# A retention layer and an MLP in one kernel, rebuilt: attention units across batches, groups of 512 with the two MLP layers in turn, Strassen products in the second layer, and gated loads

## The chip, the cores and the metric

The kernel runs on one core of one Trainium2 chip. The metric is device microseconds of one execution, as the median of several runs. An engine is named as the profile names it: PE is TensorE (PEld its weight loads), DVE is VectorE, ACT is ScalarE, POOL is GpSimd, SP is the engine that issues DMAs.

## The reference

Eight batches of 576 tokens with eight heads of 64 go through a retention layer (attention scores with a decay of gamma to the distance, causal, no softmax), and the result, as 4608 rows of 512, goes through an MLP with a leaky relu.

```python
scores = scale * np.matmul(q, k.transpose(0, 1, 3, 2))       # q, k, v: (8, 8, 576, 64) f32
gamma = 1.0 - 2.0 ** (-5.0 - np.arange(H))
Dmat = np.where(rel >= 0, gamma[:, None, None] ** rel, 0.0)  # rel = row - column
ret = scores * Dmat
attn = np.matmul(ret, v)
x = attn.transpose(0, 2, 1, 3).reshape(B * S, H * D)         # (4608, 512)
h = x @ w_in                                                 # w_in: (512, 2048)
g = np.maximum(0.01 * h, h)
return g @ w_out                                             # w_out: (2048, 512)
```

## The kernel before

Retention is computed in chunks of 64 tokens, two chunks to a unit. A unit never crosses a batch, and 576 = 4 x 128 + 64, so each batch has four full units and one of 64 rows: 40 units. For a unit, q and v are multiplied by powers of gamma (so the decay inside a block of 256 needs only a causal mask), everything is cast to f16, and q and k are transposed: on PE for units 0 to 6, by a DMA transpose from unit 7 on.

```python
def cast_qk(u):
    ...
    nc.scalar.copy(out=t[0:n, 1], in_=t32[u, 1][0:n])                       # k, on ACT
    (nc.vector if u < NEARLY else nc.gpsimd).tensor_tensor(... op=MUL)      # q times its decay
    if u >= NPE:                                                            # NPE = 7, NEARLY = 8
        nc.sync.dma_start_transpose(out=qkT[u]..., in_=t[0:n]...)
def cast_v(u):      # the same for v, DVE or POOL
...
def scores(u):      # q k^T per chunk and head, and k^T v (the chunk's state): up to 32 matmuls of 64x64
def masks(u):       # DVE: causal mask on the scores, to f16
def states(u):      # DVE: adds the chunk states up; then the cast to f16:
    (nc.scalar.copy if u < NEARLY else nc.gpsimd.tensor_copy)(out=st16[u], in_=s32)
def outputs(u):     # 32 matmuls of 64x64: own chunk ("own") and earlier chunks ("far");
    nc.scalar.copy(out=tmp..., in_=own...)                                  # ACT
    for o in range(2):
        for c in range(2):
            nc.vector.tensor_tensor(out=xT[half(o), ps, ...], in0=far..., in1=tmp..., op=ADD)
```

From unit 7 on, one step does the burst of one unit and the casts of the unit two ahead:

```python
def steady(n):
    def go():
        if NRING < n + 4 < NU:
            loads(n + 4, nc.sync)
        if n < NU:
            scores(n)
        if n > NFIRST:
            outputs(n - 1)
        if n < NU:
            masks(n)
            states(n)
        casts(n + 2)
```

The MLP works on groups of tokens, three of 256, seven of 512 and one of 256. The first layer of a group is interleaved with the second layer of the group before, and steps are spread over them so that the group after has its x in time. All matmuls of the MLP have 128x128 weights; the second layer streams 512 columns.

```python
sizes = [256] * 3 + [512] * 7 + [256]
...
def g1_blocks(g):           # first layer: hps += w_in[:, c, f]^T xT, leaky relu on ACT to f16
def g2_blocks(g, width=1):  # second layer:
    ...
    nc.tensor.matmul(out=y_cur[g, tb], lhsT=g_tiles[g][:, f, tb * P : (tb + 1) * P],
                     rhs=w_out16[:, f, :], start=(f == 0), stop=(f == NF - 1))
    ...
    nc.vector.tensor_copy(out=osb, in_=y_cur[g, tb])
    nc.sync.dma_start(out=out[r0 : r0 + P, :], in_=osb)
...
run(ends[3], g1[2] + g2_blocks(2))
run(ends[4], g1_blocks(3))
for g in range(4, NG):
    run(ends[g + 1], g1_blocks(g), g2_blocks(g - 1))
run(ends[NG], g2_blocks(NG - 1))
```

The first 12 units and the weights are loaded almost wholly from POOL's queue, in the order of its instructions (the weights are cast from f32 to f16 on the way), the later units from SP's.

Of the kernel before, what the change touches and what calls it, by code (L numbers as in the profile page):

```python
# [12 lines left out]
ADD = mybir.AluOpType.add  # L13
PSUM = bass.MemoryType.PSUM
# [3 lines left out]
def kernel(  # L18
# [9 lines left out]

# [10 lines left out]
    XR = NT // 2  # L51
# [3 lines left out]
    tab = np.zeros((P, 2, 2, H))  # L55
    for w in range(2):
        r = (P * w + np.arange(P))[:, None] - BLK / 2
        tab[:, w, 0] = gamma[None, :] ** r * scale
        tab[:, w, 1] = gamma[None, :] ** (-r)
# [9 lines left out]
    NTAB = 2 * 2 * H  # L69
# [3 lines left out]
    a_pool = ctx.enter_context(tc.tile_pool(name="ap", bufs=4))  # L73
    g_pool = ctx.enter_context(tc.tile_pool(name="gp", bufs=2))
    o_pool = ctx.enter_context(tc.tile_pool(name="op", bufs=4))
    sc_pool = ctx.enter_context(tc.tile_pool(name="scp", bufs=1, space=PSUM))
    ot_pool = ctx.enter_context(tc.tile_pool(name="otp", bufs=1, space=PSUM))
    h_pool = ctx.enter_context(tc.tile_pool(name="hpp", bufs=2, space=PSUM))
    y_pool = ctx.enter_context(tc.tile_pool(name="yp", bufs=2, space=PSUM))

    ctx.enter_context(tc.manual_schedule())

    cs = const_pool.tile([P, consts.shape[1]], FP, name="cs")
    ident = const_pool.tile([P, P], F16, name="ident")
    nc.scalar.dma_start(out=cs, in_=c_dram.ap())
    nc.scalar.dma_start(out=ident, in_=i_dram.ap())
    tab_sb = cs[:, 0:NTAB].rearrange("p (w x h) -> p w x h", w=2, x=2)
# [3 lines left out]
    xT = const_pool.tile([P, NP, XR], F16, name="xT")  # L91
    w_in16 = const_pool.tile([P, NP, DFF], F16, name="w_in16")
    w_out16 = const_pool.tile([P, NF, DM], F16, name="w_out16")
    zst = const_pool.tile([P, NP, CH], F16, name="zst")

    units = [(b, w) for b in range(B) for w in range((S + P - 1) // P)]
    NU = len(units)
    nrows = [min(P, S - P * w) for b, w in units]
    NPE = 7
    NFIRST = 7  # L100
    NEARLY = 8
    NRING = 11
    t32 = {}
    qk16 = {}
    v16 = {}
    qkT = {}
    s16s = {}
    st16 = {}
    carry = {}
# [4 lines left out]
    def swap(p):  # L114
        return 1 if p >= NP // 2 else 0

    def load(u, x, eng):
        b, w = units[u]
        n = nrows[u]
        t = ld_pool.tile([P, H, D], FP, name=f"t32_{x}")  # L120
        t32[u, x] = t
        eng.dma_start(  # L122
            out=t[0:n],
            in_=(q, k, v)[x][b, :, P * w : P * w + n, :].rearrange("h t d -> t h d"),
        )

    def loads(u, eng):
        for x in (1, 0, 2):
            load(u, x, eng)

    def cast_qk(u):

        if u >= NU:
            return
        b, w = units[u]
        n = nrows[u]
        t = a_pool.tile([P, 2, H, D], F16, name="qk16")
        qk16[u] = t
        nc.scalar.copy(out=t[0:n, 1], in_=t32[u, 1][0:n])  # L139
        (nc.vector if u < NEARLY else nc.gpsimd).tensor_tensor(  # L140
            out=t[0:n, 0],
            in0=t32[u, 0][0:n],
            in1=tab_sb[0:n, w % 2, 0, :].unsqueeze(2).to_broadcast([n, H, D]),
            op=MUL,
        )
        if u >= NPE:
            qkT[u] = a_pool.tile([P, 2, NP, P], F16, name="qkT")
            nc.sync.dma_start_transpose(  # L148
                out=qkT[u][:, :, :, 0:n].rearrange("p x c t -> p (x c) t"),
                in_=t[0:n].rearrange("t x h d -> t (x h d)"),  # L150
            )

    def cast_v(u):
        if u >= NU:
            return
        b, w = units[u]
        n = nrows[u]
        t = a_pool.tile([P, H, D], F16, name="v16")
        v16[u] = t
        (nc.vector if u < NEARLY else nc.gpsimd).tensor_tensor(  # L160
            out=t[0:n],
            in0=t32[u, 2][0:n],
            in1=tab_sb[0:n, w % 2, 1, :].unsqueeze(2).to_broadcast([n, H, D]),
            op=MUL,
        )

    def casts(u):
        cast_qk(u)
        cast_v(u)

    def transposes(u, pool=None):

        n = nrows[u]
        qkT[u] = a_pool.tile([P, 2, NP, P], F16, name="qkT")
        if pool is None:
            trs = [y_pool.tile([P, NP, P], F16, name="yps") for x in range(2)]
        else:
            both = pool.tile([P, 2, 2 * NP, P], F16, name="sc")
            trs = [both[:, x, 0:NP, :] for x in range(2)]
        for x in (1, 0):  # L180
            for p in range(NP):
                nc.tensor.transpose(  # L182
                    trs[x][:, p, 0:n],
                    qk16[u][0:n, x, 2 * p : 2 * p + 2, :].rearrange("t h d -> t (h d)"),
                    ident[0:n, 0:n],
                )
            (nc.scalar.copy if x else nc.vector.tensor_copy)(
                out=qkT[u][:, x, :, 0:n], in_=trs[x][:, :, 0:n]
            )

    sc_tiles = {}

    def scores(u):

        nb = nrows[u] // CH
        a = sc_pool.tile([P, 2, 2, NP, CH], FP, name="sc")
        sc_tiles[u] = a
        for p in range(NP):
            for g in range(2):
                for j in range(nb):  # L200
                    nc.tensor.matmul(  # L201
                        out=a[half(j), g, 0, p, :],
                        lhsT=qkT[u][half(g), 1, p, half(j)],
                        rhs=qkT[u][half(g), 0, p, half(j)],
                        start=True, stop=True, skip_group_check=True,
                    )
        if nb == 2:
            for p in range(NP):
                for j in range(2):
                    for g in range(2):  # L210
                        nc.tensor.matmul(  # L211
                            out=a[half(g), j, 1, p, :],
                            lhsT=qk16[u][half(j), 1, 2 * p + g, :],
                            rhs=v16[u][half(j), 2 * p + g, :],
                            start=True, stop=True, skip_group_check=True,
                        )

    def masks(u):
        n = nrows[u]
        s16s[u] = a_pool.tile([P, 2, NP, CH], F16, name="s16")  # L220
        nc.vector.tensor_tensor(  # L221
            out=s16s[u][0:n],
            in0=sc_tiles[u][0:n, :, 0],
            in1=mask_sb[0:n].unsqueeze(1).unsqueeze(1).to_broadcast([n, 2, NP, CH]),
            op=MUL,
        )

    def states(u):
        b, w = units[u]
        if nrows[u] < P:  # L230
            return
        st = sc_tiles[u][:, :, 1]
        s32 = a_pool.tile([P, 2, NP, CH], FP, name="s32")
        if w == 0:
            nc.vector.tensor_copy(out=s32[:, 0], in_=st[:, 0])
        else:
            nc.vector.tensor_tensor(out=s32[:, 0], in0=st[:, 0], in1=carry[b], op=ADD)
        if w % 2 == 0:
            nc.vector.tensor_tensor(out=s32[:, 1], in0=st[:, 1], in1=s32[:, 0], op=ADD)
        else:  # L240
            tmp = a_pool.tile([P, NP, CH], FP, name="stmp")
            nc.vector.tensor_tensor(out=tmp, in0=st[:, 1], in1=s32[:, 0], op=ADD)
            nc.vector.tensor_tensor(  # L243
                out=s32[:, 1], in0=tmp,
                in1=gblk_sb.unsqueeze(2).to_broadcast([P, NP, CH]), op=MUL,
            )
        carry[b] = s32[:, 1]
        st16[u] = a_pool.tile([P, 2, NP, CH], F16, name="st16")
        (nc.scalar.copy if u < NEARLY else nc.gpsimd.tensor_copy)(out=st16[u], in_=s32)  # L249

    def st_before(u, j):
        if j:
            return st16[u][:, 0]
        return st16[u - 1][:, 1] if units[u][1] else zst

    def outputs_acc(u):

        n = nrows[u]
        b, w = units[u]
        ot = ot_pool.tile([P, 2, 2 * NP, CH], FP, name="ot")  # L260
        o_all = ot[:, 0].rearrange("q (p j) t -> q p j t", j=2)
        seen = set()
        for r in range(2):
            if r:
                nc.tensor.drain()
            for p in range(NP):
                for hh in range(2):
                    o = hh ^ swap(p)
                    nc.tensor.matmul(
                        out=o_all[half(o), p, r, :],  # L270
                        lhsT=v16[u][half(r), 2 * p + hh, :],
                        rhs=s16s[u][half(r), hh, p, :],
                        start=o not in seen, stop=False, skip_group_check=True,
                    )
                    seen.add(o)
            for j in range(2):
                if w == 0 and j == 0:
                    continue
# [347 lines left out]
```

## Time and profile before

| What | Value |
|---|---|
| median of 3 runs | 337.14 us (334.98 to 345.53) |
| span of the profiled run | 337.3 us |
| PE busy | 299.5 us, 89% |
| DVE, ACT, POOL busy | 147.8, 135.6, 122.0 us |
| bytes moved by DMA | 50.32 MB |
| first-layer matmuls (L428) | 704, of which 256 stream 256 columns |
| second-layer matmuls (L451, L496) | 512 and 64, all of 512 columns |

A page of the profile gives the busy time of each engine, the span in 40 slices with a digit of tenths for each engine, the DMA queues, the chain of work that ended last, and the costliest groups of instructions by line of the kernel. In a timeline, a line has a start, a duration, the engine and line, what is written and read, and a count; "[2.11 <-DMA qkT<-qk]" means that the engine had idled for 2.11 us until that DMA landed. Matmuls are pipelined, so their durations overlap: the pace is read from the distance of starts. "issue" in a chain is time in which the engine waited for nothing that the profile shows.

### The profile page before, as it was taken

How to read it: one execution, taken by the hardware profiler on the slowest of the kernel's cores; microseconds unless marked ns; L12 is line 12 of the kernel's file. 1: busy time of each engine (PE TensorE's matmuls, PEld its weight loads, DVE VectorE, ACT ScalarE, POOL GpSimd, SP SyncE). 2: the span in 40 equal slices, each digit the busy share in tenths (PEclk: the TensorE clock that was granted, in tenths of full speed). 3: DMA queues.
4: the chain of work that ended last, by engine and by line, in shares of the span. 5: the costliest groups of instructions: out<-in, count | busy, mean ns of one | idle time of the engine just before them, and what ended most of it. 6: DMA issues, size and time to landing. Idle time of an engine off the chain costs nothing.

```text
span 337.3 us, 8449 instructions
## 1 busy us (share of the span) xinstructions
PE 299.5 (89%) x3578; PEld 154.7 (46%) x3578; DVE 147.8 (44%) x326; ACT 135.6 (40%) x240; POOL 122.0 (36%) x148
## 2 busy tenths in 40 slices
PE   1798887595775699999999999999999999999995
PEld 0476643263332344444444444444444444445652
DVE  2670444945564336434453556354436553101011
ACT  3355631164153454444453545444444433332220
POOL 8786745605355333530540355035413510000000
PEclk9999799989997779999999999999999999999999
DMA  7999999879999986866779599968697211000111
GB/s 175 214 194 189 228 231 178 197 150 176 165 244 198 162 161 142 175 144 165 160 139 192 130 189 210 217 148 158 149 214 109 66 47 61 35 33 31 62 64 62
DMA packets 122982, 50.32 MB, mean 149 GB/s; under 512 B 112192, under 2 KB 116288, under 8 KB 122944
## 3 DMA queue, kind: packets, MB, share of 16 engines
q1 hardware_dynamic: 115632, 37.11, 54.8%
q0 software_dynamic: 7024, 12.59, 19.6%
q8 instruction: 28, 0.46, 0.6%
q10 hardware_dynamic: 288, 0.08, 0.1%
q14 instruction: 10, 0.08, 0.1%
HBM read 36.78 MB, written 9.44 MB: 137 GB/s over the span
## 4 chain that ended last, share of the span: by engine, by line
PE 65%; DMA 13%; issue 10%; POOL 9%; SPq 1%; DVE 0%; POOLq 0%
PE yps L451 31%; PE hps L428 29%; DMA t<-in_v_dram 6%; DMA w_out<-in_moe_w_out_dram 5%; POOL t L122 3%; POOL v L160 2%; POOL qk L140 2%; DMA qkT<-qk 2%; PE sc L201 2%; POOL w_in L343 2%; PE ot L313 1%; PE ot L303 1%; PE sc L211 1%; SPq L122 1%; SPq L148 0%
## 5 line engine op out<-in xcount | busy, mean ns | idle before, releaser
L428 PE MATMUL hps<-xT,w_in 128*128 128x512 f16 (+1 forms) x704 | 151.2, 352 | 3.6 <-DVE osb L505 3.4
L435 ACT ACTIVATE gt<-hps 128x512 f16<-128x512 f32 x144 | 85.6, 596 | 128.0 <-PE hps L428 127.8
L451 PE MATMUL yps<-w_out,gt 128*128 128x512 f16 x512 | 127.9, 379 | 0.0
L428 PEld LDWEIGHTS <-w_in 128*128 128x128 f16 x704 | 68.8, 101 | 62.7 <-issue 9.6
L327 DVE TENSOR_TENSOR xT<-ot,own 64x256 f16<-64x256 f32 (+1 forms) x144 | 50.3, 388 | 85.8 <-ACT own L321 85.3
L451 PEld LDWEIGHTS <-gt 128*128 128x128 f16 x512 | 49.1, 98 | 56.4
L249 POOL CAST st<-s 128x512 f16<-128x512 f32 x25 | 15.3, 610 | 135.3 <-DVE s L243 68.6
L461 DVE COPY osb<-yps 128x512 f32<-128x512 f32 x32 | 21.9, 687 | 69.9 <-PE yps L451 69.9
L321 ACT COPY own<-ot 128x512 f32<-128x512 f32 (+1 forms) x36 | 19.4, 538 | 38.2 <-PE ot L313 34.8
L140 POOL TENSOR_TENSOR qk<-t,cs 128x512 f16<-128x512 f32 (+1 forms) x32 | 33.4, 1043 | 0.1
L160 POOL TENSOR_TENSOR v<-t,cs 128x512 f16<-128x512 f32 (+1 forms) x32 | 33.4, 1042 | 0.0
L221 DVE TENSOR_TENSOR s<-sc,cs 128x512 f16<-128x512 f32 (+1 forms) x40 | 27.5, 689 | 5.0 <-PE sc L211 4.0
L139 ACT CAST qk<-t 128x512 f16<-128x512 f32 (+1 forms) x40 | 24.7, 620 | 7.4 <-DMA t<-in_k_dram 7.4
L201 PE MATMUL sc<-qkT 64*64 64x64 f16 x576 | 13.5, 205 | 14.6 <-DMA qkT<-qk 11.2
L201 PEld LDWEIGHTS <-qkT 64*64 64x64 f16 x576 | 9.0, 113 | 30.5 <-DMA qkT<-qk 17.2
L182 PE MATMUL yps<-ident,qk 128*128 128x128 f16 (+1 forms) x48 | 5.9, 274 | 11.3 <-ACT qk L139 8.4
L140 DVE TENSOR_TENSOR qk<-t,cs 128x512 f16<-128x512 f32 (+1 forms) x8 | 7.9, 986 | 18.0 <-DMA t<-in_q_dram 18.0
L313 PE MATMUL ot<-qkT,st 64*64 64x64 f16 x456 | 11.8, 197 | 2.2 <-ACT st L249 1.6
L303 PE MATMUL ot<-s,v 64*64 64x64 f16 x512 | 11.7, 197 | 0.3 <-DVE s L221 0.3
L122 POOL DMA_DIRECT2D t<-in_q_dram x12 | 10.5, 877 | 3.8 <-DVE qk L140 1.9
L122 POOL DMA_DIRECT2D t<-in_v_dram x12 | 10.2, 851 | 4.3 <-DMA t<-in_k_dram 1.5
L182 PEld LDWEIGHTS <-qk 128*128 128x128 f16 (+1 forms) x56 | 4.4, 119 | 16.1 <-ACT qk L139 11.1
(42 smaller groups left out, 152.8 us busy)
## 6 DMA issues: line engine op xcount, KB each, us to landing
out_dram<-osb SPq DMA_DIRECT2D x36, 256.0 KB, 2.3
t<-in_k_dram SPq DMA_DIRECT2D x23, 256.0 KB, 3.8
t<-in_q_dram SPq DMA_DIRECT2D x22, 256.0 KB, 4.5
t<-in_v_dram SPq DMA_DIRECT2D x22, 256.0 KB, 4.8
t<-in_q_dram POOLq DMA_DIRECT2D x10, 256.0 KB, 7.8
t<-in_v_dram POOLq DMA_DIRECT2D x10, 256.0 KB, 8.2
t<-in_k_dram POOLq DMA_DIRECT2D x9, 256.0 KB, 8.0
w_in<-in_moe_w_in_dram POOLq DMA_DIRECT2D x16, 128.0 KB, 6.0
```

The costliest lines, as they stand in the source:

```text
L122: eng.dma_start(out=t[0:n], in_=(q, k, v)[x][b, :, P * w : P * w + n, :].rearrange("h t d -> t h d"),)
L139: nc.scalar.copy(out=t[0:n, 1], in_=t32[u, 1][0:n])
L140: (nc.vector if u < NEARLY else nc.gpsimd).tensor_tensor(out=t[0:n, 0], in0=t32[u, 0][0:n], in1=tab_sb[0:n, w % 2, 0, :].unsqueeze(2).to_b ...
L160: (nc.vector if u < NEARLY else nc.gpsimd).tensor_tensor(out=t[0:n], in0=t32[u, 2][0:n], in1=tab_sb[0:n, w % 2, 1, :].unsqueeze(2).to_broa ...
L201: nc.tensor.matmul(out=a[half(j), g, 0, p, :], lhsT=qkT[u][half(g), 1, p, half(j)], rhs=qkT[u][half(g), 0, p, half(j)], start=True, stop=T ...
L221: nc.vector.tensor_tensor(out=s16s[u][0:n], in0=sc_tiles[u][0:n, :, 0], in1=mask_sb[0:n].unsqueeze(1).unsqueeze(1).to_broadcast([n, 2, NP, ...
L321: nc.scalar.copy(out=tmp[:, :, 0:nb, :], in_=own[:, 0:nb].rearrange("q j p t -> q p j t"))
L327: nc.vector.tensor_tensor(out=xT[half(o), ps, t0 : t0 + n].rearrange("q p (j t) -> q p j t", t=CH), in0=far[half(o), o ^ c, :, 0:nb, :], i ...
L428: nc.tensor.matmul(out=hps[:, f, :], lhsT=w_in16[:, c, fc * P : (fc + 1) * P], rhs=xT[:, c, t0 % XR : t0 % XR + tok], start=(c == 0), stop ...
L435: nc.scalar.activation(out=g_tiles[g][:, fb * nf : (fb + 1) * nf, :], in_=hps, func=mybir.ActivationFunctionType.Lrelu,)
L451: nc.tensor.matmul(out=y_cur[g, tb], lhsT=g_tiles[g][:, f, tb * P : (tb + 1) * P], rhs=w_out16[:, f, :], start=(f == 0), stop=(f == NF - 1),)
L461: nc.vector.tensor_copy(out=osb, in_=y_cur[g, tb])
```

## The change

The kernel is written anew around the same helpers. It consists of five parts.

1. Units are 128 tokens of the flat sequence of 4608 tokens, 36 of them. A unit may hold the last chunk of one batch and the first of the next; the table of decays has a row for each such kind, and the last chunk's state isn't kept. The pairs of heads are laid out so that one DVE instruction adds "far" and "own" for a unit.
2. Every group is 512 tokens, four units. A group's first layer runs in full, then its second layer; the bursts of the units that the next group needs stand at fixed places between.
3. The second layer of groups 1 to 8 is a Strassen product (in Winograd's form): g (512 x 2048) and w_out (2048 x 512) are cut into 2 x 2 parts, and seven products of 256 x 1024 by 1024 x 256 take the place of eight. The sums of w_out's parts are made once, the sums of g's parts for each group, both on DVE in f16. Group 0 does its second layer as before.
4. All units are loaded from SP's queue, all weights from POOL's, and each queue has loads that wait for a load of the other ("behind").
5. PE does the transposes up to unit 9.

What it is for: fewer columns through PE in the second layer, fewer and larger instructions on the other engines, and a start in which weights and units land in the order of their use.

```diff
-    units = [(b, w) for b in range(B) for w in range((S + P - 1) // P)]
-    NPE = 7
+    NG = NT // TOK
+    NU = NT // P
+    NPE = 10
...
+    def behind(dma, *others):          # dma starts after others have landed
...
+    load(4, w_in_loads[2])
+    o_loads = [load_w_out(0, (last_load[4, 0],)), load_w_out(1)]
+    load(5, o_loads[0])
+    o_loads += [load_w_out(2, (last_load[5, 0],)), load_w_out(3)]
...
+    load(6, o_loads[2])
...
-        for o in range(2):
-            for c in range(2):
-                nc.vector.tensor_tensor(out=xT[half(o), ps, ...], in0=far..., in1=tmp..., op=ADD)
+        nc.vector.tensor_tensor(out=xT[g]..., in0=ot_tiles[u][:, :, NP : 2 * NP]..., in1=owns[u]..., op=ADD)
...
+    def mix(g, n, x):                  # x: half of the 8 blocks, 4 x 256 elements
+        z, a, b, op = (
+            (s[:, 0], g_part(g, 1, 0), g_part(g, 1, 1), ADD),
+            (s[:, 1], s[:, 0], g_part(g, 0, 0), SUB),
+            (g_part(g, 1, 0), g_part(g, 0, 0), g_part(g, 1, 0), SUB),
+            (g_part(g, 0, 0), g_part(g, 0, 1), s[:, 1], SUB),
+        )[n]
+        nc.vector.tensor_tensor(out=z[:, fs], in0=a[:, fs], in1=b[:, fs], op=op)
...
+        def product(name, lhs, rhs, fresh):     # 16 matmuls of 256 columns
+            ...
+            for n, (f, tb) in enumerate(order):
+                nc.tensor.matmul(out=r[name][:, tb, :], lhsT=lhs[:, f, tb * P : (tb + 1) * P],
+                                 rhs=rhs[:, f, :], start=fresh and n == 0, stop=f == HF - 1, ...)
...
+        plan = (
+            ("p1", g_part(g, 0, 0), w_part(0, 0), True, lambda: keep("k1", "p1")),
+            ("p1", g_part(g, 0, 1), w_part(1, 0), False, lambda: give(0, 0, "p1")),
+            ("p6", s[:, 1], w_mix[:, 1], True, lambda: keep("u2", "p6", "k1")),
+            ("p5", s[:, 0], w_mix[:, 0], True, lambda: keep("v", "p5", "u2")),
+            ("p7", g_part(g, 1, 0), w_mix[:, 2], True, lambda: give(1, 1, "p7", "v")),
+            ("p5", g_part(g, 0, 0), w_part(1, 1), False, lambda: give(0, 1, "p5", "u2")),
+            ("p7", g_part(g, 1, 1), w_mix[:, 3], False, lambda: give(1, 0, "p7", "u2", 2 if last else 1)),
+        )
...
+    def step(u):
+        burst(u)                       # scores(u), outputs(u - 1), masks, states, state cast, add
+        fetch(u + 3)
+        ahead(u + 2)                   # casts (k on ACT, q and v on POOL) and the DMA transpose
...
+    for g in range(2, NG):
+        more = g < NG - 1
+        for n, f in enumerate(first + second):
+            h_block(g, f)
+            if more and n in (4, 12):
+                step(4 * g + 5 + (n == 12))
+            if n == 8:
+                for m in range(3):
+                    mix(g, m, 0)
+        for m in range(3):
+            mix(g, m, 1)
+        seven(g, {0: [lambda: step(4 * g + 7)], 4: [lambda: step(4 * g + 8)]} if more else {}, g == NG - 1)
```

In the plan, a product with True starts a fresh accumulator and one with False adds to what stands in PSUM, after the reading of it that is named there ("keep" copies to SBUF, "give" to the output rows; with two names it adds on DVE, with one it copies on ACT). Before group 2, the order is written out by hand: units 0 to 3 with PE transposes, the first layer of group 0 in pieces as w_in's quarters arrive, its second layer in four parts as w_out's quarters arrive, with units 4 and 5 between them; then the first layer of group 1 with units 6 to 10.

## The prediction

> **What bounds the kernel now.** I read the page's busy table and slices first, then the windows by stage, then the PE timeline for the pace of each kind of matmul, and last the chain of waits where PE has holes.
>
> ```profile
> PE 299.5 (89%) x3578; PEld 154.7 (46%) x3578; DVE 147.8 (44%) x326; ACT 135.6 (40%) x240; POOL 122.0 (36%) x148
> PE   1798887595775699999999999999999999999995
> PEclk9999799989997779999999999999999999999999
> GB/s 175 214 194 189 228 231 178 197 150 176 165 244 198 162 161 142 175 144 165 160 139 192 130 189 210 217 148 158 149 214 109 66 47 61 35 33 31 62 64 62
> ```
>
> The reader is to see two stages. From slice 15 on (a slice is 8.4 us) PE never drops below 9; before it PE has holes, at a clock that is mostly full. The windows put the border at 116 us:
>
> ```profile
> 72.00:116.00 44.00, 29.44 (x596) 16.48 (x600) 23.57 (x57) 18.28 (x34) 19.68 (x22) 0.95 1.14 179
> 116.00:337.00 221.00, 217.36 (x2288) 104.64 (x2276) 90.17 (x202) 88.70 (x156) 55.62 (x63) 0.99 0.59 126
> ```
>
> (Columns: busy PE, PEld, DVE, ACT, POOL, granted clock, DMA share, GB/s.) After 116 us the end is set by PE alone: 217 of 221 us, and the rest is the last store. So what counts there is the pace of a matmul. Starts in the timeline of PE give it:
>
> ```profile
> 306.35 1.04 PE L428 MATMUL hps<-xT,w_in 128*128 128x256 f16 x8
> 307.22 1.89 PE L451 MATMUL yps<-w_out,gt 128*128 128x512 f16 x8
> 308.95 1.04 PE L428 MATMUL hps<-xT,w_in 128*128 128x256 f16 x8
> ```
>
> Eight matmuls of 256 columns take 307.22 - 306.35 = 0.87 us, 109 ns each, and eight of 512 take 1.73 us, 216 ns each. Each has its own weight load (PE and PEld both count 3578), so a load of 128 columns hides even behind 256. The burst of one attention unit:
>
> ```profile
> 194.96 1.03 PE L451 MATMUL yps<-w_out,gt 128*128 128x512 f16 x4
> 195.92 0.32 PE L201 MATMUL sc<-qkT 64*64 64x64 f16 x16
> ...
> 196.56 1.04 PE L428 MATMUL hps<-xT,w_in 128*128 128x512 f16 x4
> ```
>
> Four matmuls from 194.96 end their issue at 195.82; the next starts at 196.56. A burst of 64 small matmuls costs 0.73 us.
>
> Before 116 us the chain of waits is another one:
>
> ```profile
> 80.80 1.00 POOL v L160
> 81.80 4.01 issue
> 85.83 0.08 POOL st L249
> 86.40 1.04 POOL qk L140
> 87.44 1.00 POOL v L160
> 88.44 4.14 issue
> ```
>
> ```profile
> 85.83 0.61 POOL L249 CAST st<-s 128x512 f16<-128x512 f32 x1 [4.03 <-DVE s L239]
> 87.59 0.32 PE L201 MATMUL sc<-qkT 64*64 64x64 f16 x16 [2.11 <-DMA qkT<-qk]
> ```
>
> It is a loop through a unit's stations: POOL casts q and v (2.1 us), SP issues the DMA transpose (median 1.26 us, 3.3 us to landing), PE does the scores, DVE masks and states, POOL's state cast waits for DVE, and POOL's next casts stand behind it. Score bursts start at 72.1, 76.7, 82.2, 87.6 and on to 115.4: 5.4 us a unit. The MLP work placed between them, 40 matmuls of 256 columns and 76 of 512, is 4.4 + 16.4 = 20.8 us, with nine bursts 27 us of the 44. By 116 us the old kernel has scored 17 units, about 2,000 tokens, though its MLP has finished 768 and is in the first layer of the next 512. The loss is run-ahead: attention at its loop's pace with too little MLP between.
>
> **What the Trainium skill says.** "TensorE: Matmul & The Clock Gate", section "Back-to-back issue gap", gives N/2.4 + 2.5 ns for warm matmuls: 109.2 ns at 256 columns and 216 at 512, which is what the trace shows (109, 216). The same section's 131 ns for N=512 in a stream with weight loads is contradicted by the 216. "VectorE: DVE Perf Modes", section "The perf-mode tier table (the rule you actually need)", has tensor_tensor at twice the rate when all operands are 16-bit in SBUF (1224 ns for 2048 elements), once otherwise; the trace has only f32 or PSUM forms, 690 ns for 512 elements. From that page I estimate 0.69 us for a 1024-element f16 add or subtract, and 1.22 us if the fast mode fails. "DMA: Bandwidth & Descriptors", section "Issuing engines are not separate DMA queues", says that queues of different engines share the same 16 DMA engines; so the two cross-gated queues bring order, not bandwidth. The trace has both queues active in the first 60 us at about 200 GB/s, and doesn't separate them.
>
> **The change, part by part.**
>
> Strassen in the second layer: a group of 512 tokens was 64 matmuls of 512 columns, 64 x 216 = 13.8 us. It becomes seven products of 16 matmuls of 256 columns, 112 x 109 = 12.2 us. This holds for groups 1 to 8: 8 x 1.6 = 13 us less on PE, all on the path. It adds on DVE per group eight f16 sums of 1024 elements (8 x 0.69 = 5.5 us, estimate) and changes four evictions (2.8 us) to two on ACT and five on DVE (3.5 us). DVE per group is then 4 units of some 2.4 us (mask 0.69, states about 1.0, one add 0.69 where there were four of 0.42) = 9.6, + 5.5 + 3.5 = 18.6 us of 29. ACT has 16 x 0.60 + 4 x (0.62 + 0.59) + 2 x 0.59 = 15.6 us. Both fit beside PE. Latency: the first Strassen operand is needed in the third product, 1.7 + 0.7 (burst) + 1.7 = 4.1 us after the last first-layer matmul; one leaky relu (0.6) and two sums (1.4) need about 2.3 with waits. The second product adds into the PSUM of the first, so it must wait for the copy of it (0.59 on ACT and about 0.3 of latency); the burst between covers 0.7. I book 0.3 us of stall per group, 0.9 in the last, which has no burst.
>
> 36 units for 40: four fewer small casts and masks, but the 64-row units were cheap on PE (2240 small matmuls become 2304). Nothing is gained on PE; POOL and DVE lose some 4 x 2 us of work off the path.
>
> Groups of 512 with two units of lookahead: a group needs four bursts. PE per group 13.85 + 12.2 + 4 x 0.73 + 0.3 = 29.2 us, that is 7.3 us a unit, longer than the 5.4 us of the old loop, so the loop should no longer show. This is the second gain.
>
> Start: units 0 to 3 (3.15 MB) by 18 us as before. w_in follows in quarters, but on POOL they stand behind its casts and a state cast, so I put the four landings at about 20, 24, 28 and 30 us. Unit 4 is gated behind w_in's third quarter (landed 33), w_out's quarters land at 35, 38, 41 and 44, with unit 5 between. POOL must reach w_out's last issue, which is gated by unit 5's k, before it casts v of unit 4, so scores of unit 4 come near 40 us. From there come 64 matmuls of 512 (13.8 us) and two to three bursts and transposes: group 0 done at 57 us (63 before, from the last of its wide matmuls).
>
> Group 1: 13.9 + 12.2 us of matmuls, seven bursts (5.1), transposes of four units on PE (2.2) = 33 us. Here DVE does q's cast (0.69) and a transpose eviction (0.42) as well: about 24 us with the sums of weights against PE's 20 before the products. I book 6 us of waits: 39 us.
>
> Sum: 57 + 39 + 6 x 29.2 (groups 2 to 7) + 27 (group 8: 13.85 + 12.2 + 0.9) + 3.9 (last matmul to end, as before: 333.4 to 337.3) = 302 us.
>
> **Rivals.** (1) DMA becomes the bound. A unit brings 0.79 MB of loads, 0.26 of transpose and 0.26 of stores: 1.31 MB in 7.3 us = 180 GB/s for over 200 us. Slices of before show 214 to 244, so it fits; but stretches with transposes show 179. At 170 GB/s a unit takes 7.7 us, 24 units 10 us more: 312. (2) DVE's fast mode fails, or in-order DVE delays the sums: 1.22 us each brings DVE to 23 of 29 us, and the third product would wait for its operand in some groups, 1 to 2 us each: 310 to 315. (3) Narrow matmuls lose their pace in the products, because two PSUM halves alternate or weight loads surface: at 130 ns each 8 x 112 x 21 ns = 19 us more, 321. The trace's 109 ns with a load for each speaks against it. (4) The start goes worse: loads are gated by completions, some 2 us each, and PE's in-order stream stands behind any late cast: up to 10 us more. For a better result: group 1 without waits, 296.
>
> **Range and chances.** The dense part (202 us for groups 2 to 8) rests on measured paces; the first 96 us are a schedule in my head. Rivals 1, 2 and 4 each have perhaps one chance in five and cost about 10 us. So 302 us, 8 times in 10 between 293 and 317. Even two rivals together leave it below 330, hence faster by over 2% 0.94, within 0.03, slower 0.03.
>
> **What would show it.** PE at 9 in every slice from about slice 13 on; product matmuls starting 109 ns apart; groups 29 us apart in score bursts of every fourth unit; 1024-element f16 sums at 0.69 us; group 0's wide matmuls ending near 57 us and the first product near 83; no "PE <- DMA qkT" waits after 100 us. Wrong, if the chain of waits runs through DMA loads or DVE sums after 100 us, if the products show over 115 ns a matmul, or if the holes only move from 70-116 us into group 1.

## The result, and the profile after

The changed kernel takes 323.56 us (median of 4 runs, 322.8 to 324.2), against 337.19 for the kernel before: a ratio of 0.961, with a 95% interval of 0.956 to 0.966. It is faster, but by 14 us where the prediction had 35, and it lies above the predicted range. The profiled run has a span of 322.1 us, and 323.91 us as its time. Where one execution of a run was over 1.5% longer at a lower granted clock, the ratios leave it out, and in the run with casts ahead, whose profile fell on it, the median does too and no stage is read. Busy time and slices of the page of the changed kernel (a slice is now 8.05 us):

```profile
PE 283.8 (88%) x4063; PEld 192.1 (60%) x4063; DVE 171.9 (53%) x288; ACT 145.7 (45%) x255; POOL 94.7 (29%) x114
PE   2777926998757799999999999999999999999995
PEclk9997985999999999999999999999999999999999
GB/s 184 220 75 174 129 207 134 222 263 243 2 132 93 190 172 242 168 137 263 184 107 166 258 166 135 163 285 156 122 263 158 147 192 123 2 4 132 0 0 132
```

The second half looks as predicted. The first doesn't: slice 5 falls to a 2, where the prediction had continuous work on group 0, slices 10 to 13 hold 7, 5, 7, 7, and PE is full only from slice 14 on (112.7 us); group 2 starts at 117 us, as late as the dense stage of the kernel before (116). The windows by stage (columns: stage, its length, busy PE, PEld, DVE, ACT, POOL, granted clock, DMA share, GB/s): the first is the first layer of group 0, the second PE's hole, the third the second layer of group 0, the fourth group 1, the last groups 2 to 7:

```profile
23.40:42.60 19.20, 17.03 (x184) 14.16 (x185) 3.05 (x6) 10.87 (x20) 4.31 (x7) 0.91 0.90 149
42.60:51.50 8.90, 0.00 (x0) 0.00 (x0) 0.00 (x0) 0.99 (x2) 2.55 (x3) 0.68 0.92 165
51.50:70.20 18.70, 17.99 (x184) 8.33 (x184) 6.59 (x12) 2.58 (x5) 3.10 (x4) 0.88 1.07 219
70.20:117.20 47.00, 35.13 (x690) 28.99 (x689) 38.30 (x60) 21.01 (x38) 18.83 (x19) 1.00 0.66 145
117.20:291.60 174.40, 174.20 (x2561) 115.89 (x2560) 104.72 (x176) 88.25 (x153) 57.87 (x67) 1.00 0.70 162
```

The reader is to see three things. Groups 2 to 7 take 174.4 us, 29.07 each (predicted 29.2), with PE busy throughout. Group 0 ends at 70.2 us (predicted 57), with 8.9 us in which PE does nothing, and a clock of 0.88 in the stage after. Group 1 takes 47.0 us (46.8 from the first start to the first start of group 2; predicted 39), and DVE is busy for 38.3 of them. These two stages are the whole miss, 13.2 + 7.8 = 21.0 us. The other terms of the predicted sum came to 1.0 us less than predicted (174.4 for groups 2 to 7, 27.1 for group 8 and 3.6 for the rest), and 302.1 + 21.0 - 1.0 is the span of 322.1.

The pace of the products, from starts in the timeline of PE:

```profile
142.63 1.92 PE L429 MATMUL acc<-w_out,gt 128*128 128x256 f16 x16
144.39 1.91 PE L429 MATMUL acc<-w_mix,gt 128*128 128x256 f16 x16
146.14 1.03 PE L327 MATMUL acc<-xT,w_in 128*128 128x512 f16 x4
```

Sixteen matmuls of 256 columns take 1.75 us, 109 ns each, as in the first layer of the kernel before.

The hole at 42.6 us, in the timeline of POOL and in PE's:

```profile
37.92 1.52 POOL L149 DMA_DIRECT2D w_out<-in_moe_w_out_dram  x2 [10.39 <-DMA t<-in_q_dram]
48.93 1.48 POOL L149 DMA_DIRECT2D w_out<-in_moe_w_out_dram  x2 [9.49 <-DMA t<-in_q_dram]
50.42 1.06 POOL L172 TENSOR_TENSOR v<-t,cs 128x512 f16<-128x512 f32 x1
...
51.54 0.43 PE L217 MATMUL sc<-v,qk 64*64 64x64 f16 x16 [8.95 <-POOL v L172]
```

POOL stands for 10.4 us before w_out's first quarter, until q of unit 4 has landed, and for 9.5 us before the third, until q of unit 5 has. Only then does it cast v of unit 4, for which PE waits.

In group 1, these are PE's waits of over 0.3 us, in order of time:

```profile
76.75 0.40 PE L193 MATMUL acc<-ident,qk 128*128 128x128 f16 x4 [1.05 <-ACT qk L165]
82.98 0.40 PE L193 MATMUL sc<-ident,qk 128*128 128x128 f16 x4 [1.32 <-ACT qk L165]
84.06 0.38 PE L193 MATMUL sc<-ident,qk 128*128 128x128 f16 x4 [0.67 <-ACT qkT L200]
89.61 0.40 PE L193 MATMUL sc<-ident,qk 128*128 128x128 f16 x4 [1.20 <-ACT qk L165]
91.09 0.40 PE L193 MATMUL sc<-ident,qk 128*128 128x128 f16 x4 [1.08 <-DVE qk L168]
94.92 0.32 PE L208 MATMUL sc<-qkT 64*64 64x64 f16 x16 [1.69 <-DVE qkT L200]
102.03 0.32 PE L208 MATMUL sc<-qkT 64*64 64x64 f16 x16 [1.62 <-DMA qkT<-qk]
108.64 1.03 PE L429 MATMUL acc<-w_mix,gt 128*128 128x256 f16 x8 [0.55 <-DVE w_mix L394]
110.09 1.03 PE L429 MATMUL acc<-w_mix,gt 128*128 128x256 f16 x8 [0.41 <-DVE w_mix L394]
113.53 1.91 PE L429 MATMUL acc<-w_out,gt 128*128 128x256 f16 x16 [1.77 <-DVE v L443]
```

With one short wait more (0.18 us, for DVE) they add up to 5.7 us for DVE, 4.2 for ACT (casts of k and copies of PE's transposes) and 1.6 for the DMA transpose of unit 11. What held DVE up is in the chain of waits:

```profile
88.18 1.40 DVE w_mix L394 x2
89.58 1.45 DVE qk L168
91.03 1.46 DVE mix L413
...
107.89 4.19 DVE w_mix L394 x4
112.08 0.61 DVE u L443
```

From 88 us the chain runs through DVE: sums of w_out's parts (w_mix, two and four of them in one line), a cast of q, sums of g (mix), and the first of two additions behind which PE's sixth product starts (at 113.53). The sum of g at 91.03 takes 1.46 us where 0.69 was estimated.

### The profile page after: what moved, and what is told of

Read it like the earlier page. It is cut to its first block, busy times and chain, and to the rows that moved or that the text cites. A ratio compares the mean times of both kernels' runs of the same rounds, so it can differ in the third digit from the quotient of the medians.

```text
span 322.1 us, 9343 instructions
## 1 busy us (share of the span) xinstructions
PE 283.8 (88%) x4063; PEld 192.1 (60%) x4063; DVE 171.9 (53%) x288; ACT 145.7 (45%) x255; POOL 94.7 (29%) x114
## 3 DMA queue, kind: packets, MB, share of 16 engines
q1 hardware_dynamic: 145152, 44.58, 59.2%
## 4 chain that ended last, share of the span: by engine, by line
PE 75%; DVE 9%; DMA 7%; ACT 3%; issue 3%; POOL 1%; SPq 1%; DVEq 0%; POOLq 0%; ACTq 0%
PE acc L327 33%; PE acc L429 28%; PE acc L369 5%; DMA t<-in_q_dram 4%; PE sc L208 2%; DMA w_in<-in_moe_w_in_dram 2%; DMA w_out<-in_moe_w_out_dram 2%; DVE w_mix L394 2%; PE sc L217 1%; PE acc L193 1%; PE ot L284 1%; PE ot L295 1%; DVE mix L413 1%; ACT qkT L200 1%; DVE s L250 1%
## 5 line engine op out<-in xcount | busy, mean ns | idle before, releaser
L327 PE MATMUL acc<-xT,w_in 128*128 128x512 f16 (+1 forms) x704 | 131.5, 344 | 2.4 <-DMA w_in<-in_moe_w_in_dram 2.4
L341 ACT ACTIVATE gt<-acc 128x512 f16<-128x512 f32 x144 | 86.1, 598 | 66.4 <-PE acc L327 64.8
L226 DVE TENSOR_TENSOR s<-sc,cs 128x512 f16<-128x512 f32 x36 | 24.7, 686 | 46.3 <-PE sc L217 46.2
L429 PE MATMUL acc<-w_out,gt 128*128 128x256 f16 x384 | 45.9, 273 | 2.7 <-DVE v L443 1.8
L172 POOL TENSOR_TENSOR v<-t,cs 128x512 f16<-128x512 f32 x36 | 40.7, 1132 | 6.1 <-DMA t<-in_v_dram 6.1
L429 PE MATMUL acc<-w_mix,gt 128*128 128x256 f16 x256 | 30.7, 273 | 1.0 <-DVE w_mix L394 1.0
L314 DVE TENSOR_TENSOR xT<-ot,own 128x512 f16<-128x512 f32 x36 | 24.6, 685 | 11.8 <-ACT own L306 11.7
L429 PE MATMUL acc<-w_mix,mix 128*128 128x256 f16 x256 | 29.3, 273 | 0.0
L168 POOL TENSOR_TENSOR qk<-t,cs 128x512 f16<-128x512 f32 x26 | 28.5, 1095 | 0.0
L429 PEld LDWEIGHTS <-mix 128*128 128x128 f16 x256 | 25.1, 98 | 2.9
```

The costliest lines, as they stand in the source:

```text
L168: eng.tensor_tensor(out=qk16[u][:, 0], in0=t32[u, 0], in1=decay(u, 0), op=MUL)
L172: eng.tensor_tensor(out=v16[u], in0=t32[u, 2], in1=decay(u, 1), op=MUL)
L226: nc.vector.tensor_tensor(out=s16s[u], in0=sc_tiles[u][:, :, 0], in1=mask_sb.unsqueeze(1).unsqueeze(1).to_broadcast([P, 2, NP, CH]), op=MUL,)
L314: nc.vector.tensor_tensor(out=xT[g][:, :, t0 : t0 + P].rearrange("q (c g) t -> q c g t", g=2), in0=ot_tiles[u][:, :, NP : 2 * NP].rearrang ...
L327: nc.tensor.matmul(out=hps[:, n, :], lhsT=w_in16[:, c, f * P : (f + 1) * P], rhs=xT[g][:, c, ts], start=(c == 0), stop=(c == NP - 1),)
L341: nc.scalar.activation(out=out, in_=in_, func=mybir.ActivationFunctionType.Lrelu)
```

## The experiments

The theory after the result has three parts: (1) POOL's order and the gates make the hole in group 0; (2) DVE binds group 1, with the sums of weights in it; (3) POOL's casts slow DVE's sums. The rivals: the bytes of the start bind; round trips between engines bind group 1; the products themselves cost what they save. All runs but one compute the same output; the one is said. Stages are read from the starts of PE's matmuls in one profiled execution: "end of group 0" is the first matmul of group 1's first layer. The last column is what blocks of 16 matmuls of 256 columns in group 1 took beyond their usual 1.91 us: where it isn't 0, the granted clock of group 1 was 0.93 to 0.97, and elsewhere 1.00. What lowered the clock there no run shows, so these parts are not counted for or against an edit.

| Run | median us | end of group 0 | group 1 | of it, lower clock |
|---|---|---|---|---|
| changed kernel | 323.56 | 70.2 | 46.8 | 0 |
| v of unit 4 on DVE | 319.82 | 64.8 | 48.0 | 2.4 |
| five gates left out | 315.05 | 59.2 | 48.8 | 1.5 |
| sums of weights early, one block | 323.23 | 72.6 | 43.7 | 1.2 |
| groups 2 to 8 without products | 335.29 | 69.8 | 46.8 | 0 |
| no gates, sums of weights spread | 309.37 | 59.8 | 42.5 | 0 |
| casts of units 8 to 12 on ACT | 319.18 | 69.8 | 42.8 | 0 |
| no gates, sums spread, group 1 plain | 310.25 | 60.0 | 41.4 | 0 |
| no gates, sums spread, casts ahead | 309.68 | not read | not read | |
| no gates, sums spread, w_in early | 305.08 | 55.3 | 44.0 | 1.4 |
| the same with casts ahead | 305.29 | 55.1 | 43.1 | 1.1 |
| no gates, w_in early, no products at all | 314.42 | 56.4 | 41.0 | 0 |

**v of unit 4 on DVE.**

```diff
-    cast_v(4, nc.gpsimd)
+    cast_v(4, nc.vector)
```

> One instruction moves: the cast of v of unit 4 goes from POOL to DVE, so it no longer stands behind the two gated issues of w_out. Theory A (the 9 us hole of PE at 42.6 us is POOL's instruction order): the hole goes; PE then runs wide matmuls until it needs w_out's third quarter, which still lands near 55 us, and waits there 3 to 4 us; group 0 ends at 63 to 65 us in place of 70.2 and the whole time falls by 5 to 7 us (the colder clock after the hole, 2 us, included), to about 317. Rival B (the start is bound by the bytes that must land, so the hole is only where the wait shows): group 0 still ends at 68 or later and the time falls by 2 us or less.

Measured: 319.82 us, 3.7 less. The hole is gone, and the timeline of PE shows the wait that was named in its place:

```profile
50.72 1.03 PE L369 MATMUL acc<-w_out,gt 128*128 128x512 f16 x4
55.21 1.10 PE L369 MATMUL acc<-w_out,gt 128*128 128x512 f16 x4 [3.46 <-DMA w_out<-in_moe_w_out_dram]
```

Group 0 ends at 64.8 us, 5.4 earlier and within the expectation; group 1 is 1.2 longer, by its lower clock (2.4), so the whole gained less than expected. The hole was POOL's order, not the bytes; but behind it stands w_out, late because of its gates.

**Five gates left out.**

```diff
-    load(4, w_in_loads[2])
-    o_loads = [load_w_out(0, (last_load[4, 0],)), load_w_out(1)]
-    load(5, o_loads[0])
-    o_loads += [load_w_out(2, (last_load[5, 0],)), load_w_out(3)]
+    load(4)
+    o_loads = [load_w_out(0), load_w_out(1)]
+    load(5)
+    o_loads += [load_w_out(2), load_w_out(3)]
...
-    load(6, o_loads[2])
+    load(6)
```

> The five gates between the two queues after w_in (on the loads of units 4, 5 and 6 and on the first and third quarter of w_out) are left out; the first gate of w_in stays. Theory A (the gates cost more than their order brings: each is a round trip with DMA idle behind it, and the gate on POOL holds up the cast): no hole at 42.6 us, w_in lands 2 to 5 us later, w_out entire by 48 us, group 0 ends at 60 to 64 us, the time falls by 6 to 10 us. Rival B (the gates are needed: without them units 4 to 9 flood the DMA engines and w_in comes late): first-layer matmuls of group 0 have holes of 8 us or more, and the time is the same or longer.

Measured: 315.05 us, 8.5 less. PE's timeline:

```profile
25.62 3.38 PE L327 MATMUL acc<-xT,w_in 128*128 128x256 f16 x16 [2.90 <-DMA w_in<-in_moe_w_in_dram]
...
42.87 6.22 PE L369 MATMUL acc<-w_out,gt 128*128 128x512 f16 x28
...
59.20 1.91 PE L327 MATMUL acc<-xT,w_in 128*128 128x256 f16 x16
```

The first matmul of the MLP comes 2.2 us later than with the gates (25.6 for 23.4): w_in is issued as before (16.8 us, 17.3 with the gates), but now beside the loads of units 4 to 6, which SP issues from 12.5 us on. Everything after is on time: no hole at 42.6, no wait for w_out, group 0 done at 59.2. Between 25.6 and 42.8 us the DMA engines move 201 GB/s; with the gates it was 149 between 23.4 and 42.6. The rival, that the gates are needed, falls.

**Sums of weights early, in one block** (all eight in group 0's second layer, six of them behind the last add).

```diff
+    mix_weights(0, 0)
+    mix_weights(0, 1)
     wides((3, 1), (0, 2))
...
     finish(5)
+    for n in range(1, 4):
+        mix_weights(n, 0)
+        mix_weights(n, 1)
```

> The eight sums of w_out's parts move from group 1, where DVE is busy without a gap, to group 0's second layer, where DVE and POOL are idle. Theory A (group 1 is bound by DVE): 8 instructions of 0.7 to 1.5 us leave it (7.1 us busy), group 1 takes 41 us in place of 47.0, the time falls by 4 to 7 us, to about 317, and the sums take 0.69 us each in their new place. Rival B (group 1 is bound by round trips of PE with ACT and DVE for each unit, in order): group 1 falls by 2 us or less.

Measured: 323.23 us, the same. But the sums were put in DVE's stream in front of the evictions of group 0:

```profile
72.56 3.16 PE L327 MATMUL acc<-xT,w_in 128*128 128x256 f16 x16 [2.15 <-DVE osb L379]
```

PE waited 2.15 us for an accumulator, and its first 16 matmuls then took 3.16 us, not 1.91. Group 1 itself took 43.7 us, 3.1 less. The run doesn't decide; the gain and the new wait cancel.

**Groups 2 to 8 without products** (64 matmuls of 512 columns, no sums of g).

```diff
-        seven(
+        plain(
             g,
             {0: [lambda: step(4 * g + 7)], 4: [lambda: step(4 * g + 8)]} if more else {},
```

> Groups 2 to 8 do their second layer as 64 matmuls of 512 columns, with no sums of g; group 1 keeps its products. Theory A (the products of 256 columns keep their pace, and the sums are hidden): a group takes 13.8 + 13.8 + 2.9 = 30.6 us in place of 29.1, the last one 27.7 in place of 27, and the time rises by 9 to 11 us. Rival B (the products lose at PE, or through waits for sums and copies, what they save in columns): the time is the same within 3 us.

Measured: 335.29 us, 11.7 more; the ratio to the kernel before is 0.993 (0.986 to 1.000). PE's timeline gives the group:

```profile
116.61 4.48 PE L327 MATMUL acc<-xT,w_in 128*128 128x512 f16 x20
...
147.22 1.03 PE L327 MATMUL acc<-xT,w_in 128*128 128x512 f16 x4
```

30.61 us, against 29.07 with products. So a group gains 1.54 us where its columns promise 1.6, and the products earn 7 x 1.54 = 10.8 us in groups 2 to 8; the 11.7 of the medians has the scatter of the runs in it (332.86 to 336.53 here). Nearly all that the changed kernel gained was theirs: without them it is the kernel before within the interval, 2 us apart, though group 1 still has its products in this run.

**No gates, and the sums of weights spread** over gaps of DVE.

```diff
     cast_q(5, nc.vector)
+    for n in range(2):
+        mix_weights(n, 0)
+        mix_weights(n, 1)
...
     add(4)
+    mix_weights(2, 0)
+    mix_weights(2, 1)
...
     transposed(6, 0, nc.vector.tensor_copy)
+    mix_weights(3, 0)
...
     transposed(7, 0, nc.vector.tensor_copy)
+    mix_weights(3, 1)
```

> The kernel without the five gates (which took 315.05 us), and in it the eight sums of w_out's parts spread over gaps of DVE from 44 us on: four behind the cast of q of unit 5, two behind the add of unit 4, one each behind the transposes of units 6 and 7, none in front of an eviction that PE needs. The run that moved them in one block was the same as the changed kernel, but there they stood before the four evictions of group 0 and PE waited for those. Theory A (DVE's time binds the second half of group 1): group 1 falls from 48.8 us to 43 to 45, the whole to 309 to 312 us. Rival B (round trips of the units bind it): 313 to 316 us.

Measured: 309.37 us, 5.7 less than without gates alone; group 1 fell from 48.8 to 42.5, 4.8 us if the lower clock of the former is taken off. PE's waits for DVE in group 1 fell from 6.0 to 1.2 us, and those for ACT rose from 4.3 to 5.4. This is what the block had hidden: the sums of weights stood on group 1's path.

**Casts of units 8 to 12 on ACT** (the changed kernel; the multiplication by the decay is left out for these units, so the output is another).

```diff
+        if eng is nc.gpsimd and 8 <= u <= 12:
+            nc.scalar.copy(out=qk16[u][:, 0], in_=t32[u, 0])
+            return
...
+        if eng is nc.gpsimd and 8 <= u <= 12:
+            nc.scalar.copy(out=v16[u], in_=t32[u, 2])
+            return
```

> The changed kernel with the casts that POOL does for units 8 to 12 (v of all five, q of 10 to 12) as plain copies on ACT; the multiplication by the decay is left out for these, so the output is another. It tells whether DVE's sums are slowed by POOL's two-operand instructions beside them. Theory A (they share a way to SBUF): the f16 sums and the q cast that took 1.3 to 1.5 us between 88 and 105 us take 0.69, DVE is 5 us less busy in group 1, and group 1 falls by 3 to 5 us from 47.0, the whole to 319 to 321 us. Rival B (the long ones are long by their own operands): they stay at 1.3 to 1.5 us, and the time is the same within 2 us.

Measured: 319.18 us, 4.4 less; group 1 fell from 46.8 to 42.8. PE's waits for DVE there fell from 5.7 to 2.2 us and that for the transpose of unit 11 from 1.6 to 0.2, while those for ACT, which has the casts now, rose from 4.2 to 5.8. So DVE is most of the gain, and an earlier transpose is part of it. DVE's timeline at the same place, first in the changed kernel, then in this run:

```profile
89.50 1.52 DVE L168 TENSOR_TENSOR qk<-t,cs 128x512 f16<-128x512 f32 x1
90.95 1.53 DVE L413 TENSOR_TENSOR mix<-gt 128x1024 f16<-128x1024 f16 x1
92.52 1.41 DVE L413 TENSOR_TENSOR mix<-mix,gt 128x1024 f16<-128x1024 f16 x1
```

```profile
89.07 0.68 DVE L171 TENSOR_TENSOR qk<-t,cs 128x512 f16<-128x512 f32 x1
89.67 0.68 DVE L419 TENSOR_TENSOR mix<-gt 128x1024 f16<-128x1024 f16 x1
90.39 0.69 DVE L419 TENSOR_TENSOR mix<-mix,gt 128x1024 f16<-128x1024 f16 x1
```

The same instructions on the same operands take less than half without POOL's multiplications beside them. POOL pays too: in the changed kernel its casts take 1.48 us there, 1.04 alone.

```profile
89.00 1.48 POOL L168 TENSOR_TENSOR qk<-t,cs 128x512 f16<-128x512 f32 x1
```

The Trainium skill has the rule, on a page that the prediction didn't draw on ("SBUF — State Buffer", section "Who interferes with whom"): a DVE instruction with two SBUF inputs contends with a GpSimd instruction that reads SBUF. The trace agrees on which instructions collide: DVE's instructions with one operand in PSUM keep their 0.69 us (a mask at 98.10, beside a POOL cast from 98.18). The section speaks of an exclusive lock; here neither of the pair kept its own pace, both took longer, 1.52 and 1.48 us.

The profile of the kernel before had the collision too, once, and the prediction passed over it: DVE's one cast of q beside POOL's casts, and the cast of v after them:

```profile
61.80 3.06 DVE L140 TENSOR_TENSOR qk<-t,cs 128x512 f16<-128x512 f32 x1
64.78 0.68 DVE L160 TENSOR_TENSOR v<-t,cs 128x512 f16<-128x512 f32 x1
```

POOL ran four casts of 1.03 to 1.05 us without a gap from 60.27 to 64.30; DVE's cast ended 0.56 us after the last of them, so there POOL kept its pace and DVE stood, as the section has it.

**Group 1 plain as well** (no gates, sums of weights spread; group 1 with 64 matmuls of 512 columns and no sums of g).

```diff
-    for n in range(3):
-        mix(1, n, 0)
...
-    seven(1, {0: [lambda: step(11)], 1: [rest_of_weights], 4: [lambda: step(12)]})
+    plain(1, {0: [lambda: step(11)], 4: [lambda: step(12)]})
```

> The kernel without gates and with the early sums of weights, and group 1 does its second layer as 64 matmuls of 512 columns too: 1.6 us more on PE, eight sums of g and one eviction less on DVE. Theory A (DVE binds group 1): the sums of g were 8 to 10 us of DVE there, so group 1 falls below that of the run with products in group 1 by 2 to 4 us in spite of the longer matmuls, to 40 to 42 us, the whole to 306 to 309 us. Rival B (PE and its round trips bind it): 1 to 2 us longer than with the products.

Measured: 310.25 us (308.32 to 312.46) against 309.37 (309.18 to 311.68): no difference that these runs show. Group 1 is 1.1 us shorter in the profiled run, half of the least that theory A had: PE is busy for 35.7 us in place of 34.3, and its waits are 5.6 us in place of 8.1. What the products save there in columns they lose in waits: 1.5 us for the transpose of unit 11, which stands behind a shorter first product, and 1.0 for DVE. 5.4 of the 5.6 are waits for ACT.

**Casts ahead** (on the kernel without gates and with spread sums: casts and DMA transposes of units 10 to 12 one burst earlier, with five buffers) and **w_in early** (on the same kernel as casts ahead: the last gate left out too, and w_in's quarters issued behind the v casts of units 1, 2 and 3). First casts ahead, then w_in early:

```diff
-    a_pool = ctx.enter_context(tc.tile_pool(name="ap", bufs=4))
+    a_pool = ctx.enter_context(tc.tile_pool(name="ap", bufs=5))
...
+    ahead(10)
     halves(1, (0, 6), (0, 7))
...
-    ahead(10)
...
+    ahead(11)
     halves(1, (1, 4), (1, 5))
...
-    ahead(11)
+    fetch(13)
+    ahead(12)
     halves(1, (1, 6), (1, 7))
```

```diff
+        w_in_loads.append(load_w_in(u - 1))
+        if u == 3:
+            w_in_loads.append(load_w_in(3))
         finish(u - 1)
-        if u == 2:
-            w_in_loads.append(load_w_in(0, (last_load[2, 2],)))
-        if u == 3:
-            w_in_loads.append(load_w_in(1))
...
-    w_in_loads.append(load_w_in(2))
-    w_in_loads.append(load_w_in(3))
```

> The kernel without gates and with early sums of weights (309.37 us; group 1 took 42.5 us there), and in it the casts and DMA transposes of units 10 to 12 one burst earlier than before, with five buffers in place of four for the attention tiles and the loads of units 12 and 13 earlier to suit. Two things remain in group 1 by my reading: sums of g beside POOL's casts (1.4 to 1.5 us each in place of 0.69, about 5 us in all), and a wait of 1.5 us for the transpose of unit 11. Theory A: part of the casts now runs where DVE reads PSUM, the wait goes, group 1 falls to 38.5 to 40.5 us and the whole to 305 to 307.5. Rival B (the chain through PE, ACT and DVE per unit binds, POOL doesn't): within 1 us of 309.4.

> The kernel without gates and with early sums of weights, and the last gate (w_in's first quarter behind unit 2) left out too, the issues of w_in's quarters right behind the v casts of units 1, 2 and 3 on POOL, not behind a state cast. Theory A (w_in is late because POOL issues it late: its first matmul waits 2.2 us and the second piece 1.5 us): first-layer matmuls begin at 22 to 23 us in place of 25.2 and have no hole of over 1 us, the whole falls by 2 to 4 us to 305.5 to 307.5. Rival B (the bytes bind: w_in earlier makes units 2 and 3 later by as much): the same within 1 us.

> Both of the last two edits together, the version that I expect to beat both kernels. If the stages are independent, the gains add: 302 to 304.5 us. If the second only moves the start of a stage that is bound by loads of units, no more than the better of the two.

Casts ahead: 309.68 us (307.68 to 311.61) against 309.37 without, as its rival had it. Together with w_in early it took 305.29 against 305.08 without: the 2 to 4 us of theory A aren't there. The timeline of DVE for the run with both shows why in part:

```profile
68.33 1.49 DVE L168 TENSOR_TENSOR qk<-t,cs 128x512 f16<-128x512 f32 x1
```

The wait for the transpose of unit 11 is gone, and the later sums of g take 0.69; but POOL's earlier casts now meet the q cast of unit 8, on which PE waits, and group 1 is only 0.9 us shorter. Moving the collision is not removing it.

W_in early: 305.08 us, 4.3 less, a little more than theory A had. PE's timeline:

```profile
22.55 1.91 PE L327 MATMUL acc<-xT,w_in 128*128 128x256 f16 x16
...
55.28 1.91 PE L327 MATMUL acc<-xT,w_in 128*128 128x256 f16 x16
```

In group 1 of this profile, 16 matmuls ran at a lower clock (the first lines). The same ones behind the same waits in the run with the late w_in did not (the second):

```profile
69.51 0.58 PE L193 MATMUL sc<-ident,qk 128*128 128x128 f16 x4 [0.67 <-ACT qkT L200]
69.89 3.30 PE L327 MATMUL acc<-xT,w_in 128*128 128x256 f16 x16
```

```profile
74.07 0.38 PE L193 MATMUL sc<-ident,qk 128*128 128x128 f16 x4 [0.67 <-ACT qkT L200]
74.29 1.91 PE L327 MATMUL acc<-xT,w_in 128*128 128x256 f16 x16
```

So group 1 is no longer by the edit than the 42.5 us above; the 1.5 more are its clock.

This is the best version: 305.08 us, a ratio of 0.908 to the kernel before (0.905 to 0.912), and it beats the changed kernel by 18 us with order alone.

**No products at all**, on that start.

> The best start so far (no gates, w_in issued early, 305.08 us with products) and no Strassen product in any group: all nine groups as 64 matmuls of 512 columns, no sums of w_out or g. It separates the two gains that the prediction added up. Theory A (the products are worth 11 to 12 us and the new order of units and groups is worth the rest of the 20 that the prediction gave it, once its start is mended): 7 x 1.6 us more in groups 2 to 8 and about 0 in group 1, 315.5 to 318 us, so the new order alone is 18 to 20 us faster than the kernel before. Rival B (the mended start only helps together with the products): over 322 us.

Measured: 314.42 us, a ratio of 0.934 (0.927 to 0.940). The new order alone, with its start mended, is 22 us faster than the kernel before; the products add 9.3 (314.42 - 305.08). In the two profiles groups 2 to 8 are 10.7 us shorter with products, but group 1 is 3.0 longer (44.0 for 41.0), where the columns alone would have made it 1.6 shorter. The waits of PE are 2.9 us longer (8.1 for 5.2: 1.5 more for the transpose of unit 11, 1.0 for DVE, 0.4 for ACT), and 1.4 are the lower clock of that profile.

## Why the prediction was wrong, step by step

**Right.** The pace of the narrow matmuls (109 ns), a group's 29.2 us (29.07), the stage of groups 2 to 8 (202 us predicted; 117.0 to 318.5 is 201.5), the worth of the products in these groups (1.6 us each predicted, 1.54 measured; the eighth of the 13 us, group 1, gave nothing), and 0.69 us for an f16 sum as long as POOL is quiet. Rival 1, DMA as the bound, and rival 3, products that lose their pace, are both refuted: 162 GB/s with PE busy for 174.2 of 174.4 us.

**Wrong: the start.** The step that failed is "scores of unit 4 come near 40 us", in the paragraph on the start; they were complete at 51.5. It had the right mechanism, POOL behind gated issues of w_out, and mis-sized the gates. I took loads to follow one another at the rate of bytes, though each gate waits for a landing: unit 4 started at 32.4 (behind w_in's third quarter, which I had at 28), w_out's first quarter at 37.9, unit 5 at 43.7, w_out's third quarter at 48.9, that is 5 to 6 us a link where I had about 3. I also read the gate on w_out's third quarter as unit 5's k; it is its q, issued 0.4 us later (44.08 for 43.66). Of the 13.2 us, the order of v on POOL alone is 5.4 (first run) and all five gates are 11.0 (second run); with w_in issued earlier as well, group 0 ended at 55.3, before the predicted 57. The colder clock after the hole (28 matmuls in 8.2 us, 6.2 without the hole) wasn't in the sum at all. Rival 4 named the gates and capped them at 10 us.

**Wrong: group 1.** The step that failed is "I book 6 us of waits": PE waited 11.5 us there (5.7 for DVE, 4.2 for ACT, 1.6 for a DMA transpose) and was busy for 35.1 where the sum had 33. The prediction looked for the waits before the products, with DVE's 24 us against PE's 20. In that part DVE was busy for only 20.0 of 28.3 us (70.2 to 98.5), and PE waited longer for ACT (4.2 us), which the prediction had not named for it, than for DVE (2.9). From the first product on, where its text named no waits, DVE was busy for 18.3 of 18.7 us: half of the sums of weights and five of the eight sums of g stand there, and PE waited for two of those sums and for an addition behind them (108.64, 110.09 and 113.53). Two causes of DVE's lateness were taken out one at a time: the sums of weights (4.8 us of group 1, without the difference in clock) and the casts of POOL, beside which DVE's two-operand instructions took twice as long (4.0 us, with the earlier transpose in it). The two gains were measured apart, and they may overlap. Rival 2 named late sums on DVE, but in every group and from a failing fast mode; they were late in group 1, and the fast mode didn't fail, the neighbour slowed it, as the 3.06 us of the kernel before could have told. The prediction's last sign of being wrong came true: the holes moved into group 1, with one wait for a DMA transpose after 100 us (1.62 us at 102.03).

**Wrong by omission: how the gains add.** The prediction gave the new order some 20 us (337 - 13 - 302 = 22) and the products 13, and treated the start as a small correction. The runs show 22 for the order, but only with the start mended; as it was written, the start and group 1 gave back all of it but 2 us, which is within the scatter of the runs. So the expected gain wasn't absent: it was spent before the stage that it was meant for.

What stays open: in the best version group 1 still takes 44.0 us, 1.4 of them by the clock, against 29.1 for a later group with three bursts fewer, and PE transposes fewer. Its waits are 8.1 us: 5.4 for ACT, 1.5 for the DMA transpose of unit 11 and 1.2 for DVE. Waits for ACT of 4.2 to 5.8 us stand in group 1 of every run whose stages were read, and no edit aimed at them; so round trips between PE and ACT hold for this part, as the rival had it. What the time would gain without them isn't shown.

## What to carry to other kernels

A gate between two DMA queues costs a landing for each link, 5 to 6 us here, and a gate in the queue of an engine that also computes holds up everything behind it in that engine's order; a load order that is right by bytes is to be checked for what stands behind each wait. The gain of a new order can be that the steady stage begins earlier, and then the start is to be worked out instruction by instruction, as the steady stage was. And sums added to a half-idle engine must be placed: before or behind which eviction they stand, and beside what on POOL, decided here between 0 and 6 us.

## What the runs showed of the hardware that was not expected

DVE's two-operand instructions from SBUF took 1.41 to 1.53 us beside POOL's two-operand casts, and 0.68 to 0.69 without them; POOL's took 1.48 and 1.04. That is less than the sum of both (1.73) and more than the longer one alone. In the kernel before, a DVE cast of 0.69 us took 3.06 beside POOL casts that followed one another at 1.03 to 1.05. After 8.9 us without a matmul, PE ran the next ones of 512 columns at 288 ns each on average (28 from 51.90 to 59.97), and at 216 when there was no hole. Short waits were followed by a lower clock in one execution and not in another: behind the same wait of 0.67 us, 16 matmuls of 256 columns took 3.30 us in one run and 1.91 in another.
